# A list scheduler plans the first pass of layer one on every engine

## The chip, the cores and the metric

One core of a Trainium2 chip runs the kernel. The metric is the device time of one execution in microseconds (us), the median of several runs. Matrix products run on TensorE (PE; PEld is its weight load), reductions and elementwise work on VectorE (DVE), exponentials, tanh and copies on ScalarE (ACT). SyncE (SP) issues every DMA. Each engine works through its own queue in the order in which the program gives it.

## The reference, cut to what matters

```python
k_p = k.reshape(B, H, Sp, 8, D).mean(axis=3)          # B=8, H=8, D=64, 576 positions -> Sp=72
v_p = v.reshape(B, H, Sp, 8, D).mean(axis=3)
attn = softmax(q @ k_p.T / sqrt(D))                   # per batch and head
x = (attn @ v_p), heads side by side                  # 4608 tokens x 512
h = x @ w_in;  g = h / (1 + exp(-1.702 h));  y = g @ w_out     # layer one, d_ff 2048
out = ((y @ w_a) * (y @ w_b)) @ w_o2                  # layer two, d_ff 1536
```

The weights come in 64-bit floats and are converted on the chip into two 32-bit parts (hi, lo). Activations are split in the same way, and each product of layer one is three products, hi by hi, hi by lo and lo by hi.

## The kernel before

The 4608 tokens are 9 blocks of 512. A block has four units of 128 tokens, 36 units in all, and 4.5 units make a batch of the attention. Layer one runs in two passes over the blocks: the first takes `FIRST_FS` = 2, 3, 4, 5, 6, 6, ... chunks of 128 hidden columns of block 0, 1, 2, ..., 44 steps in all; the second pass takes the rest. A step is 12 products `h` (128x512), tanh on ACT, gate on DVE, hi on ACT, lo on DVE, and 12 products `acc` (the output y, four banks). Layer two follows. Attention for the units of a block runs in the first pass, between the steps of the block before it.

A unit's stages, with the lines of the profile: scores `sc` (PE, L286), maxima `mx` (DVE, L293), exponentials into `at` (ACT, L296), normalising (DVE, L308 to L310), transposes `pt` (PE, L318), their copies `aT` (ACT, L321), averages `px` (PE, L333), and x's hi part (ACT, L97) and lo part (DVE, L98), each in two halves of 256 columns. A batch needs the sums of k (`ks`, DVE L255, then `kbd` on ACT) and of v (`vs`, DVE L267), from loads `kraw`, `vraw` (`kvraw` for the first two batches), whose buffers are one and two. A weight chunk is loaded as `raw`, and converted on ACT and DVE (`tmp`, `w`, L120 to L139). A block's x is stored to memory (`xd`) for the second pass, in four transfers, and loaded there in four, `load_x` being issued five steps ahead.

What sets the order: the start is written out by hand (`in_order`, `keep_busy`), and from block 1's attention on, `spread` deals the attention's stages over the steps of the block before. `tc.issue_after` ties an operation to the newest DVE instruction; apart from that the framework orders an engine's instructions by its own estimate. `keep_busy(n)` issues n products of the identity with itself (`busy`, L170) so that TensorE does not stand idle:

```python
keep_busy(12)
in_order(*sk[0], b1(0)[0], b1(1)[0], b1(0)[1], b1(1)[1], *b1(2), sv[0][0])
keep_busy(8)
...
spread([o for t in ts for o in later[t]], place[0, j - 1, 0] - 1, place[0, j, 0] - 1)
```

A product of 32-bit operands (`busy`, `sc`, `px`) stands as two records in the trace; `pt` and the 128x512 products of layer one are one record each.

Of the kernel before, what the change touches and what calls it, by code (L numbers as in the profile page):

```python
# [20 lines left out]
LOW, HIGH = (struct.unpack("<f", struct.pack("<I", b))[0] for b in (0x38000000, 0x47EFFFFF))  # L21


@with_exitstack
def tile_kernel(ctx, tc, q, k, v, w_in, w_out, w_a, w_b, w_o2, out):
# [54 lines left out]
    newest = [None]  # L80

    def vec(made):
        newest[0] = made.ins
        return made

    def in_order(*ops):

        for o in ops:
            if newest[0] is None:
                o()  # L90
            else:
                with tc.issue_after(newest[0]):
                    o()

    def split(hi, lo, src):

        nc.scalar.copy(out=hi, in_=src)  # L97
        vec(nc.vector.tensor_tensor(out=lo, in0=src, in1=f32(hi), op=ALU.subtract))  # L98
# [15 lines left out]
    def convert(raw, t, hi, lo, part, first_on_act=False):  # L114
# [3 lines left out]
        if part == 0:  # L118
            if first_on_act:
                nc.scalar.activation(out=f32(t), in_=f32(high), func=AF.Abs)  # L120
            else:
                nc.vector.tensor_scalar(out=t, in0=high, scalar1=0x7FFFFFFF, scalar2=None, op0=ALU.bitwise_and)
# [5 lines left out]
            vec(nc.vector.scalar_tensor_tensor(  # L128
                out=t, in0=high, scalar=0xC0000000, in1=t, op0=ALU.bitwise_and, op1=ALU.bitwise_or
            ))  # L130
            nc.scalar.copy(out=hi, in_=f32(t))
            return
# [6 lines left out]
        vec(nc.vector.tensor_tensor(out=lo, in0=f32(t), in1=f32(low), op=ALU.add))  # L139

    def mm3(o, whi, wlo, xhi, xlo, first, last):
        nc.tensor.matmul(out=o, lhsT=whi, rhs=xhi, start=first, stop=False)  # L142
        nc.tensor.matmul(out=o, lhsT=whi, rhs=xlo, start=False, stop=False)  # L143
        nc.tensor.matmul(out=o, lhsT=wlo, rhs=xhi, start=False, stop=last)  # L144
# [74 lines left out]
    early = {}  # L219
    q_t, ks_t, vs_t, at_t, atT_t, kraw_t, vraw_t = {}, {}, {}, {}, {}, {}, {}  # L220
# [20 lines left out]


    scale = 1.0 / (POOL * D ** 0.5)

    def to_kbd(b, half, ks):


        cs = slice(2 * half, 2 * half + 2)
        nc.scalar.mul(out=kbd[b % 2][0:D, cs, 0:SP], in_=ks[0:D], mul=scale)
        nc.scalar.mul(out=kbd[b % 2][D:P, cs, SP:2 * SP], in_=ks[D:P], mul=scale)  # L250

    def sum_k(b, half):
        ks = ap_.tile([P, 2, SP], F32, tag="ks", name="ks", bufs=2)
        raw = kraw_t.pop((b, half)).rearrange("p c (s r) -> p c s r", r=POOL)
        vec(nc.vector.tensor_reduce(out=ks, in_=raw, op=ALU.add, axis=AX.X))  # L255
        to_kbd(b, half, ks)

    def load_v(b, h, n, raw=None):
        if raw is None:
            raw = ap_.tile([SP, n, D, POOL], F32, tag="vraw", name="vraw", bufs=2)  # L260
        nc.sync.dma_start(out=raw, in_=v[b, :, h:h + n])
        vraw_t[b, h] = raw

    def sum_v(b, h, n):
        if h == 0:
            vs_t[b] = ap_.tile([SP, H, D], F32, tag="vs", name="vs", bufs=2)
        vec(nc.vector.tensor_reduce(out=vs_t[b][:, h:h + n, :], in_=vraw_t.pop((b, h)), op=ALU.add, axis=AX.X))  # L267

    def stage_b1(u, half):
        qT = q_t[u]  # L270
        if half == 0:
            at_t[u] = (
                early["at"][:, u % 2] if UB > u >= UB // 2 else ap_.tile([P, H, SP], F32, tag="at", name="at", bufs=2),
# [3 lines left out]
        a, mx, sm = at_t[u]  # L277
        if (u, half) in ((2, 0), (2, 1), (3, 0)):
            sc = acc.tile([P, H // 2, SP], F32, tag="acc", name="sc")
        else:  # L280
            sc = ps.tile([P, H // 2, SP], F32, tag="ps", name="sc")
        pin = after_last if u < UB else lambda made: None
        for c in range(2):
            pair = 2 * half + c
            for o, n, b in pieces(u):
                pin(nc.tensor.matmul(  # L286
                    out=sc[o:o + n, 2 * c:2 * c + 2, :].rearrange("p h k -> p (h k)"),
                    lhsT=qT[:, pair, o:o + n],
                    rhs=kbd[b % 2][:, pair, :],
                    start=True, stop=True,  # L290
                ))
        hs = slice(half * (H // 2), (half + 1) * (H // 2))
        vec(nc.vector.tensor_reduce(out=mx[:, hs], in_=sc, op=ALU.max, axis=AX.X, negate=True))  # L293
        for c in range(H // 2):
            h = half * (H // 2) + c
            nc.scalar.activation(  # L296
                out=a[:, h, :], in_=sc[:, c, :], func=AF.Exp, bias=mx[:, h:h + 1],
                accum_out=sm[:, h:h + 1],
            )
        if half == 1:  # L300
            q_t.pop(u)
            if UB <= u + 2 < NU:
                load_q(u + 2)

    def stage_b2(u):
        a, _, sm = at_t[u]

        nc.vector.tensor_scalar(out=sm, in0=sm, scalar1=1e-9, scalar2=float(POOL), op0=ALU.add, op1=ALU.mult)  # L308
        nc.vector.reciprocal(out=sm, in_=sm)
        vec(nc.vector.tensor_tensor(out=a, in0=a, in1=sm.unsqueeze(2).to_broadcast([P, H, SP]), op=ALU.mult))  # L310

    def stage_c(u):
        a = at_t.pop(u)[0]
        aT = early["aT"][:, u // 2] if u in (1, 3) else ap_.tile([SP, H, P], F32, tag="aT", name="aT", bufs=1)
        for half in range(2):
            pt = ps.tile([SP, H // 2, P], F32, tag="ps", name="pt")
            for c in range(H // 2):
                made = nc.tensor.transpose(pt[:, c, :], a[:, half * (H // 2) + c, :], ident)  # L318
                if u < UB:
                    after_last(made)  # L320
            nc.scalar.copy(out=aT[:, half * (H // 2):(half + 1) * (H // 2), :], in_=pt)  # L321
        atT_t[u] = aT

    def stage_d(u):
        aT = atT_t.pop(u)
        j, c0 = u // UB, u % UB * P
        if (0, j) not in x_t:
            x_t[0, j] = x_tiles()
        px = ps.tile([P, NP, P], F32, tag="ps", name="px")
        for c in range(NP):  # L330
            for e in range(2):
                for o, w, b in pieces(u):
                    made = nc.tensor.matmul(  # L333
                        out=px[e * D:(e + 1) * D, c, o:o + w],
                        lhsT=vs_t[b][:, 2 * c + e, :],
                        rhs=aT[:, 2 * c + e, o:o + w],
                        start=True, stop=True,
                    )
                    if u < UB:
                        after_last(made)  # L340
        for h in range(2):
            hi, lo = x_t[0, j][0][h], x_t[0, j][1][h]
            split(hi[:, :, c0:c0 + P], lo[:, :, c0:c0 + P], px[:, 2 * h:2 * h + 2])
            if u % UB == UB - 1:
                nc.sync.dma_start(out=xd[j][:, 0, 2 * h:2 * h + 2], in_=f32(hi))
                nc.sync.dma_start(out=xd[j][:, 1, 2 * h:2 * h + 2], in_=f32(lo))
# [4 lines left out]


    def slot(t, lo, hi):

        todo = [
            (t, op(stage_b1, t, 0)), (t - 1, op(stage_b2, t - 1)), (t - 2, op(stage_d, t - 2)),
            (t, op(stage_b1, t, 1)), (t - 1, op(stage_c, t - 1)),
        ]
        return [o for u, o in todo if lo <= u < hi]

    slots = [slot(t, 0, UB) for t in range(UB + 2)]
    later = {t: slot(t, UB, NU) for t in range(UB, NU + 2)}
    V = 2
    for b in range(2, B):
        u0 = b * S // P
        for t, ops in (
            (u0 - 5, [op(load_k, b, 0)]), (u0 - 4, [op(sum_k, b, 0), op(load_k, b, 1), op(load_v, b, 0, V)]),
            (u0 - 3, [op(sum_k, b, 1), op(load_v, b, V, V)]),
            (u0 - 2, [op(sum_v, b, 0, V), op(load_v, b, 2 * V, V)]),
            (u0 - 1, [op(sum_v, b, V, V), op(load_v, b, 3 * V, V)]),  # L370
# [653 lines left out]
```

## Time and profile before

| | us |
|---|---|
| median of 3 runs | 1805.42 (1804.43 to 1808.48) |
| the profiled execution | 1805.87, its span 1804.1 |
| PE busy in the span | 1751.0 (97%) |
| DVE busy in the span | 1040.4 (58%) |
| ACT busy in the span | 607.1 (34%) |

The span is the stretch from the first to the last instruction that the profile holds; 1.8 us lie around it. Busy time of PE is modelled, so a busy PE is not PE at its best; the granted clock (PEclk) says whether it ran at its full 2.4 GHz (1.00) or at 1.2 GHz (0.50).

### The profile page before, as it was taken

What the parts mean: (1) busy time and instruction counts of PE and PEld (TensorE: products, weight loads), DVE (VectorE), ACT (ScalarE), POOL (GpSimd) and SP (SyncE); (2) the same over time, 40 slices, a digit from 0 to 9 for tenths busy, and PEclk for the clock granted to TensorE, in tenths of its full rate; (3) what the DMA queues carried; (4) which work ended last, traced back from release to release, by engine and by line L of the source; (5) the groups of instructions that cost most, each with busy time, mean ns of one, the idle gap of its engine ahead of it and who ended that gap; (6) DMA issues with size and microseconds to landing.
All of it is one profiled execution on the core that took longest, in us unless ns stands there. A gap on an engine that the chain in (4) does not pass through costs nothing.

```text
span 1804.1 us, 22540 instructions
## 1 busy us (share of the span) xinstructions
PE 1751.0 (97%) x8584; PEld 1443.2 (80%) x8584; DVE 1040.4 (58%) x1821; ACT 607.1 (34%) x1515; POOL 1.7 (0%) x8
## 2 busy tenths in 40 slices
PE   7779999999999999999999999999999999999998
PEld 6557788888888888888887788878788888788887
DVE  6877787667534768758755665733334443434343
ACT  5666665533222333323333232222221111221121
POOL 0000000000000000000000000000000000000000
PEclk8999999999999999999999999999999999999999
DMA  8475553353220644657587675768436659536612
GB/s 259 144 230 193 178 171 127 117 193 129 75 113 35 239 181 184 247 181 257 209 307 310 267 278 178 258 262 331 193 127 223 233 187 333 225 134 248 233 56 91
DMA packets 92171, 357.98 MB, mean 198 GB/s; under 512 B 10304, under 2 KB 10304, under 8 KB 71680
## 3 DMA queue, kind: packets, MB, share of 16 engines
q1 hardware_dynamic: 92064, 356.56, 54.8%
q8 instruction: 67, 1.10, 0.2%
q14 instruction: 40, 0.33, 0.1%
HBM read 238.55 MB, written 117.96 MB: 198 GB/s over the span
## 4 chain that ended last, share of the span: by engine, by line
PE 88%; DVE 5%; DMA 5%; ACT 1%; issue 0%; SPq 0%; ACTq 0%; DVEq 0%
PE X L516 16%; PE Y L516 8%; PE acc L143 7%; PE acc L144 7%; PE acc L142 7%; PE h L142 7%; PE h L144 7%; PE h L143 7%; PE acc L471 5%; PE acc L469 5%; PE acc L470 5%; PE Z L516 4%; DMA vraw<-in_v_dram 2%; PE px L333 1%; PE sc L286 1%; PE pt L318 1%
## 5 line engine op out<-in xcount | busy, mean ns | idle before, releaser
L516 PE MATMUL X<-xo,wc 128*128 128x512 f32 (+1 forms) x1440 | 330.3, 370 | 5.3 <-DVE s L534 4.5
L516 PEld LDWEIGHTS X<-xo,wc 128*128 128x128 f32 x1440 | 255.5, 189 | 58.7 <-DVE s L534 11.7
L143 PE MATMUL acc<-glo,w 128*128 128x512 f32 x576 | 227.4, 395 | 2.1 <-DVE glo L444 2.1
L142 PE MATMUL h<-x,w 128*128 128x512 f32 x576 | 225.7, 393 | 1.4 <-ACT aT L321 0.7
L144 PE MATMUL acc<-ghi,w 128*128 128x512 f32 x576 | 226.2, 394 | 0.0
L143 PE MATMUL h<-x,w 128*128 128x512 f32 x576 | 224.7, 390 | 0.0
L144 PE MATMUL h<-x,w 128*128 128x512 f32 x576 | 224.6, 390 | 0.0
L439 DVE SCALAR_TENSOR_TENSOR g<-g,h 128x512 f32<-128x512 f32 x144 | 98.5, 684 | 185.1 <-ACT g L436 185.0
L142 PE MATMUL acc<-ghi,w 128*128 128x512 f32 x576 | 176.1, 398 | 10.9 <-ACT ghi L440 7.1
L436 ACT ACTIVATE g<-h 128x512 f32<-128x512 f32 x144 | 86.2, 599 | 279.5 <-PE h L144 243.3
L516 PE MATMUL Y<-xo,wc 128*128 128x512 f32 (+1 forms) x720 | 167.4, 368 | 0.0
L501 ACT CAST ghi<-s 128x512 fp32r<-128x512 f32 (+1 forms) x60 | 34.7, 578 | 337.4 <-DVE s L535 337.4
L516 PEld LDWEIGHTS Y<-xo,wc 128*128 128x128 f32 x720 | 128.4, 189 | 23.7
L530 DVE TENSOR_TENSOR s<-s,Y 128x512 f32<-128x512 f32 (+1 forms) x60 | 38.0, 634 | 170.7 <-PE Y L516 170.3
L142 PEld LDWEIGHTS acc<-ghi,w 128*128 128x128 f32 x576 | 106.7, 189 | 33.9 <-ACT ghi L440 9.0
L143 PEld LDWEIGHTS acc<-glo,w 128*128 128x128 f32 x576 | 109.1, 189 | 25.8 <-DVE glo L444 3.0
L142 PEld LDWEIGHTS h<-x,w 128*128 128x128 f32 x576 | 108.3, 188 | 25.5 <-ACT aT L321 1.8
L144 PEld LDWEIGHTS acc<-ghi,w 128*128 128x128 f32 x576 | 109.3, 190 | 23.0 <-DVE w L139 0.6
L440 ACT CAST ghi<-g 128x512 fp32r<-128x512 f32 x144 | 89.7, 623 | 109.6 <-DVE g L439 76.9
L144 PEld LDWEIGHTS h<-x,w 128*128 128x128 f32 x576 | 108.2, 188 | 22.7 <-issue 0.2
L143 PEld LDWEIGHTS h<-x,w 128*128 128x128 f32 x576 | 108.3, 188 | 22.1 <-issue 0.2
L444 DVE TENSOR_TENSOR glo<-g,ghi 128x512 fp32r<-128x512 f32 x144 | 99.0, 687 | 36.8 <-ACT ghi L440 35.6
(90 smaller groups left out, 2521.4 us busy)
## 6 DMA issues: line engine op xcount, KB each, us to landing
xo<-yd SPq DMA_DIRECT2D x84, 1024.0 KB
yd<-st SPq DMA_DIRECT2D x28, 1024.0 KB
part<-part SPq DMA_DIRECT2D x108, 256.0 KB
xd<-x SPq DMA_DIRECT2D x36, 512.0 KB
part<-ys SPq DMA_DIRECT2D x72, 256.0 KB
x<-xd SPq DMA_DIRECT2D x36, 512.0 KB
raw<-in_moe_w_out_dram SPq DMA_DIRECT2D x28, 512.0 KB
wd<-ws SPq DMA_DIRECT2D x12, 1024.0 KB
```

Of the source, the lines that this page charges most:

```text
L142: nc.tensor.matmul(out=o, lhsT=whi, rhs=xhi, start=first, stop=False)
L143: nc.tensor.matmul(out=o, lhsT=whi, rhs=xlo, start=False, stop=False)
L144: nc.tensor.matmul(out=o, lhsT=wlo, rhs=xhi, start=False, stop=last)
L436: nc.scalar.activation(out=g, in_=hps, func=AF.Tanh, scale=0.5 * 1.702)
L439: made = vec(nc.vector.scalar_tensor_tensor(out=g, in0=g, scalar=1.0, in1=hps, op0=ALU.add, op1=ALU.mult))
L440: nc.scalar.copy(out=ghi, in_=g)
L444: return rest, lambda: vec(nc.vector.tensor_tensor(out=glo, in0=g, in1=f32(ghi), op=ALU.subtract))
L469: after_last(nc.tensor.matmul(out=oa, lhsT=chi[:, ts], rhs=whi, start=first, stop=False))
L470: after_last(nc.tensor.matmul(out=oa, lhsT=chi[:, ts], rhs=wlo, start=False, stop=False))
L471: after_last(nc.tensor.matmul(out=oa, lhsT=clo[:, ts], rhs=whi, start=False, stop=last))
L516: after_last(nc.tensor.matmul(out=banks[nm], lhsT=w[:, at_, we, ks], rhs=x[:, xe, kk, :], start=n in FIRST and kk == 0 and m == 0, stop=kk ...
L530: nc.vector.tensor_tensor(out=s[2], in0=s[2], in1=Y, op=ALU.add)
```

## The change

All work of the first pass (loads, attention, weight chunks 0 to 10, the 44 steps, their evictions and stores) becomes a table of tasks (`first_tasks`) with an engine, a cost, what it waits for, and the buffers that it takes and gives back. `first_plan` is a list scheduler in the source: it takes the task that can start earliest by its table, ties by the longest path to the end plus a bonus per kind (`LEAN`). The kernel emits the tasks in the order of the planned starts, and `pin` holds PE, ACT and DVE to that order. Up to the first y product, gaps that the plan leaves on PE are filled with `keep_busy`, six products for each us of gap (`FILL`). The copies `aT` become half buffers (three of them). x's hi and lo parts become whole tiles: one copy and one subtraction of 512 columns for each unit, a block's store and load two transfers of 1 MB in place of four. The first conversion step of chunks 6 to 10 moves from DVE to ACT, and the first three blocks' evictions are all ACT's (6 fewer on DVE in the pass).

```diff
+COST = dict(
+    k=1.51, q=.67, v=1.51, vq=.76, w=1.34, x=2.69, p=.67,
...
+DELAY = dict(PE=.30, ACT=.18, DVE=.18, SP=2.2)
+ROOM = dict(ps=4, acc=3, at=2, aT=3, tmp=2, g=1, gg=2, ks=2, kraw=1, vraw=2, q=2, xs=3, raw=2, yp=2, w=19)
...
+FILL = 6
+ACT_EVICTS = 3
...
+def first_tasks(counts, seq, chunks_made, per):
+
+    tasks = {}
+
+    def add(name, engine, kind, deps=(), takes=(), gives=()):
+        tasks[name] = (engine, kind, list(deps), list(takes), list(gives))
...
+            add(f"mx{u}.{e}", "DVE", "mx", [f"sc{u}.{e}"])
+            add(f"ex{u}.{e}", "ACT", "ex", [f"mx{u}.{e}"], (), [bank])
+        add(f"b2{u}", "DVE", "b2", [f"ex{u}.0", f"ex{u}.1"])
+        for e in range(2):
+            back = ([f"px{u - 1}.0"] if e else [f"px{u - 2}.1"]) if u >= per else [f"px{u - 2}.{e}"] if u >= 2 else []
+            add(
+                f"pt{u}.{e}", "PE", "pt", [f"b2{u}"] + back + ([f"pt{u}.0"] if e else []), [bank],
+                ([] if u == 2 else ["w"] if u == 3 else ["at"]) if e else [],
+            )
+            add(f"cp{u}.{e}", "ACT", "cp", [f"pt{u}.{e}"], ["aT"], [bank])
...
+def first_plan(tasks):
...
+        path[n] = COST[tasks[n][1]] + .2 + max([path[m] for m in after[n]], default=0.)
+    key = {n: -path[n] - LEAN.get(t[1], 0.) for n, t in tasks.items()}
+    room, ready, bank, start = dict(ROOM), {}, {}, {}
+    free = dict(PE=2.3, ACT=2.8, DVE=2.8, SP=.7)
...
+    while len(start) < len(tasks):
+        best = None
+        for e, names in queue.items():
+            for n in names:
+                s = max(free[e], ready[n], now)
+                if (best is None or (s, key[n], n) < best) and fits(tasks[n][3]):
+                    best = (s, key[n], n)
...
+        queue[engine].remove(n)
+        start[n] = s
+        free[engine] = s + COST[kind]
+        end = free[engine] + DELAY[engine]
+        for r in back:
+            heapq.heappush(gives, (end, bank[holder(n)] if r == "any" else r))
...
+    def pin(engine, made):
+
+        if engine in chain:
+            tc.add_manual_dep(
+                made.ins, chain[engine].name,
+                mybir.DependencyInfo(mybir.DependencyClass.NoSync, mybir.DependencyReason.DATA),
+                reason="order of the plan",
+            )
+        chain[engine] = made.ins
+        return made
...
     def load_x(i, j):
-        x_t[i, j] = x_tiles()
+        x_t[i, j], ts = x_tiles()
         for e in range(2):
-            for h in range(2):
-                nc.sync.dma_start(out=f32(x_t[i, j][e][h]), in_=xd[j][:, e, 2 * h:2 * h + 2])
+            nc.sync.dma_start(out=f32(ts[e]).rearrange("p h k n -> p (h k) n"), in_=xd[j][:, e])
 
...
+    def copy_aT(u, half):
+        aT_t[u, half] = ap_.tile([SP, H // 2, P], F32, tag="aT", name="aT", bufs=ROOM["aT"])
+        pin("ACT", nc.scalar.copy(out=aT_t[u, half], in_=pt_t.pop((u, half))))
...
+    def x_part(u, e):
+        j, c0 = u // UB, u % UB * P
+        if e == 0 and u % UB == 0:
+            x_t[0, j], x_full[j] = x_tiles()
+        hi, lo = (t.rearrange("p h k n -> p (h k) n")[:, :, c0:c0 + P] for t in x_full[j])
+        if e == 0:
+            pin("ACT", nc.scalar.copy(out=hi, in_=px_t[u]))
+        else:
+            pin("DVE", nc.vector.tensor_tensor(out=lo, in0=px_t.pop(u), in1=f32(hi), op=ALU.subtract))
+
+    def store_x(j, e):
+        nc.sync.dma_start(out=xd[j][:, e], in_=f32(x_full[j][e]).rearrange("p h k n -> p (h k) n"))
...
-                if c % 2 == 0:
-                    nc.scalar.mul(out=t, in_=sums[c], mul=0.5)
-                else:
-                    nc.vector.tensor_scalar_mul(t, sums[c], 0.5)
-                nc.sync.dma_start(out=part[1][j][:, c, :], in_=t)
...
-    keep_busy(12)
-    in_order(*sk[0], b1(0)[0], b1(1)[0], b1(0)[1], b1(1)[1], *b1(2), sv[0][0])
-    keep_busy(8)
-    in_order(b2(0))
-    c_(0)()
-    keep_busy(3)
-    in_order(sv[0][1], b2(1), *b1(3), b2(2), c0[0], d_(0))
...
+    n1 = place[1, 0, FIRST_FS[0]]
+    start, bank = first_plan(tasks := first_tasks(FIRST_FS, S, FA + HELD, UB))
...
+    names = sorted(does, key=len, reverse=True)
+    pe_free, filling = 2.3, True
+    for name in sorted(start, key=lambda n: (start[n], n)):
+        kind = next(k_ for k_ in names if name.startswith(k_))
+        if tasks[name][0] == "PE":
+            if kind == "y" and filling:
+                filling = False
+                busy.clear()
+            if filling:
+                keep_busy(int((start[name] - pe_free) * FILL))
+            pe_free = start[name] + COST[tasks[name][1]]
+        does[kind](*(int(n) for n in name[len(kind):].split(".")))
```

The order on PE at the start of the program. `busy` are the fill products, `qs` and `kbd` the queries and summed keys of the first units, `at` the exponentials. Before:

```order
L170 MATMUL busy<-ident 128x128 x12
L286 MATMUL sc<-kbd_135,qs 128x144 x12
L170 MATMUL busy<-ident 128x128 x8
L318 MATMUL pt<-ident,at 72x128 x8
L170 MATMUL busy<-ident 128x128 x3
L286 MATMUL sc<-kbd_135,qs 128x144 x4
L333 MATMUL px<-aT,vs 64x128 x8
```

And now:

```order
L338 MATMUL busy<-ident 128x128 x41
L466 MATMUL sc<-kbd_135,qs 128x144 x8
L338 MATMUL busy<-ident 128x128 x11
L466 MATMUL sc<-kbd_135,qs 128x144 x2
L338 MATMUL busy<-ident 128x128
L466 MATMUL sc<-kbd_135,qs 128x144 x2
L338 MATMUL busy<-ident 128x128 x12
L498 MATMUL pt<-ident,at 72x128 x4
```

The fill ahead of the first scores grows from 12 products to 41, and more stands between the first units. Ahead of the first h product the whole order holds 104 fill products where it held 32, and four more come after it; it also holds all scores of units 4 and 5 and the transposes of unit 4 there, which came after it before.

The order on DVE where the first sums of v from the small buffers `vraw` stand (batch 2). `ks` are sums of k, `mx` maxima, `sm` and `at` the normalising, `x` the lo parts. Before:

```order
L293 TENSOR_REDUCE mx<-sc 128x4
L255 TENSOR_REDUCE ks<-kraw 128x144
L293 TENSOR_REDUCE mx<-sc 128x4
L308 TENSOR_SCALAR sm<-sm 128x8
L309 RECIPROCAL sm<-sm 128x8
L310 TENSOR_TENSOR at<-at,sm 128x576
L98 TENSOR_TENSOR x<-px,x 128x2x128 x2
L293 TENSOR_REDUCE mx<-sc 128x4
L267 TENSOR_REDUCE vs<-vraw 72x128
```

And now, with `g` and `glo` of a step and `tmp` of a weight chunk among them:

```order
L528 TENSOR_TENSOR x<-px,x 128x4x128
L423 TENSOR_REDUCE ks<-kraw 128x144
L475 TENSOR_REDUCE mx<-sc 128x4
L1080 TENSOR_TENSOR glo<-g,ghi 128x512
L444 TENSOR_REDUCE vs<-vraw 72x128 x2
L1069 SCALAR_TENSOR_TENSOR g<-g,h 128x512
L475 TENSOR_REDUCE mx<-sc 128x4 x2
L584 TENSOR_SCALAR tmp<-tmp 128x512
```

The two sums now stand together between a step's lo part (`glo`) and the next step's gate (`g`), where each stood among a unit's normalising and maxima; the lo part of x is one instruction of 512 columns for a unit in place of two of 256.

The order of the loads on SP at the start. Before:

```order
L239 DMA kvraw<-in_k_dram 128x1152
L233 DMA qs<-in_q_dram 128x512
L239 DMA kvraw<-in_k_dram 128x1152
L233 DMA qs<-in_q_dram 128x512 x2
L261 DMA kvraw<-in_v_dram 72x2048 x2
L233 DMA qs<-in_q_dram 128x512
```

And now:

```order
L610 DMA raw<-in_moe_w_in_dram 128x1024
L417 DMA kvraw<-in_k_dram 128x1152 x2
L610 DMA raw<-in_moe_w_out_dram 128x1024
L409 DMA qs<-in_q_dram 128x512 x4
L409 DMA q<-in_q_dram 128x512 x2
L417 DMA kraw<-in_k_dram 128x1152
L437 DMA kvraw<-in_v_dram 72x2048
```

The first weight chunk goes ahead of k, and the first v comes behind the queries of six units.

## Rows read from the trace of the kernel before

**Rows 1.** Windows: length, busy time per engine (records), granted clock, DMA share, GB/s.

```profile
0.00:51.00 51.00, 37.81 (x235) 31.48 (x235) 34.86 (x59) 27.35 (x107) 1.73 (x8) 0.87 0.77 230
51.00:100.00 49.00, 36.23 (x260) 27.39 (x260) 38.13 (x69) 33.52 (x149) 0.00 (x0) 0.97 0.59 187
100.00:150.00 50.00, 41.65 (x296) 32.63 (x292) 40.48 (x75) 31.60 (x116) 0.00 (x0) 0.97 0.66 209
150.00:200.00 50.00, 45.84 (x267) 36.25 (x268) 38.40 (x77) 30.99 (x121) 0.00 (x0) 0.97 0.50 164
200.00:250.00 50.00, 49.04 (x313) 39.24 (x313) 36.05 (x72) 29.74 (x108) 0.00 (x0) 1.00 0.54 184
250.00:427.00 177.00, 177.00 (x1022) 145.06 (x1017) 117.84 (x237) 89.94 (x300) 0.00 (x0) 1.00 0.43 151
```

**Rows 2.** Timeline of PE, start: start, duration, records [idle before, releaser].

```profile
2.34 5.49 PE L170 MATMUL busy<-ident 128*128 128x128 f32 x24 [2.34 <-POOL ident masks.py:199]
7.62 1.06 PE L286 MATMUL sc<-kbd,qs 128*128 128x144 f32 x4
10.05 3.01 PE L286 MATMUL sc<-kbd,qs 128*128 128x144 f32 x20 [1.37 <-DMA qs<-in_q_dram]
12.90 1.95 PE L170 MATMUL busy<-ident 128*128 128x128 f32 x16
...
22.35 1.09 PE L333 MATMUL px<-aT,vs 72*64 72x128 f32 x16
23.37 1.07 PE L318 MATMUL pt<-ident,at 128*72 128x128 f32 x8
...
49.74 0.39 PE L142 MATMUL h<-x,w 128*128 128x512 f32 x1
49.97 0.40 PE L143 MATMUL h<-x,w 128*128 128x512 f32 x1
```

**Rows 3.** Waits of PE from 51 to 250: us in total, times, longest.

```profile
PE pt L318 <- DVE at L310: 11.3, 7, 3.9
PE acc L142 <- ACT ghi L440: 4.1, 3, 2.5
PE acc L142 <- ACT w L131: 3.6, 1, 3.6
```

**Rows 4.** Waits of DVE from 51 to 250.

```profile
DVE g L439 <- ACT g L436: 13.8, 7, 3.5
DVE vs L267 <- DMA vraw<-in_v_dram: 8.0, 8, 1.8
DVE ks L255 <- DMA kraw<-in_k_dram: 7.1, 3, 3.8
...
DVE ys L630 <- DMA part<-ys: 3.3, 1, 3.3
```

**Rows 5.** Chain that ended last, its DMAs from 88 to 126.

```profile
88.12 7.36 DMA vraw<-in_v_dram
96.75 9.02 DMA vraw<-in_v_dram
...
121.74 4.45 DMA kraw<-in_k_dram
```

**Rows 6.** Groups by line and shape: busy, mean ns of one | idle before.

```profile
L98 DVE TENSOR_TENSOR st<-part,st 128x512 fp32r<-128x512 f32 x63 | 41.8, 686 | 4.4 <-ACT st L97 4.2
...
L98 DVE TENSOR_TENSOR x<-px,x 128x256 fp32r<-128x256 f32 x72 | 30.0, 418 | 12.2 <-ACT x L97 11.8
...
L630 DVE TENSOR_SCALAR ys<-acc 128x512 f32<-128x512 f32 x18 | 12.4, 688 | 15.8 <-DMA part<-ys 15.5
...
L122 DVE TENSOR_SCALAR tmp<-raw 128x512 uint32<-128x512 uint32 x20 | 8.4, 421 | 0.0
L120 ACT ACTIVATE tmp<-raw 128x512 f32<-128x512 f32 x12 | 8.0, 671 | 12.1 <-DMA raw<-in_moe_w_in_dram 8.2 <-DMA raw<-in_moe_w_out_dram 2.6 <-DVE w L139 1.1
```

**Rows 7.** Windows at the start, the columns as in the first group.

```profile
0.00:10.00 10.00, 6.35 (x28) 6.10 (x28) 2.61 (x2) 2.13 (x4) 1.73 (x8) 1.00 0.80 247
10.00:20.00 10.00, 6.70 (x48) 6.27 (x49) 7.92 (x12) 8.11 (x51) 0.00 (x0) 0.93 1.02 281
```

More of the change, by code (lines that the diff above doesn't have):

```diff
@@ new lines, in holder, with fits @@
+def holder(name):
+    kind = name[:2]
+    if kind in ("sc", "ex"):
+        return "sc" + name[2:]
+    if kind in ("pt", "cp"):
+        return "pt" + name[2:]
+    return "px" + name[2:].split(".")[0]
+def first_plan(tasks):
+    after = {n: [] for n in tasks}
+    left = {n: len(t[2]) for n, t in tasks.items()}
+    for n, t in tasks.items():
+        for d in t[2]:
+            after[d].append(n)
+    todo, line = dict(left), [n for n in tasks if not left[n]]
+    for n in line:
+        for m in after[n]:
+            todo[m] -= 1
+            if not todo[m]:
+                line.append(m)
+    path = {}
+    for n in reversed(line):
+        path[n] = COST[tasks[n][1]] + .2 + max([path[m] for m in after[n]], default=0.)
+    key = {n: -path[n] - LEAN.get(t[1], 0.) for n, t in tasks.items()}
+    room, ready, bank, start = dict(ROOM), {}, {}, {}
+    free = dict(PE=2.3, ACT=2.8, DVE=2.8, SP=.7)
+    queue = {e: [] for e in free}
+    for n, t in tasks.items():
+        if not left[n]:
+            ready[n] = 0.
+            queue[t[0]].append(n)
+    now, gives = 0., []
+    def fits(takes):
+        return all(
+            room["ps"] > 0 or room["acc"] > 0 if r == "any" else room[r] >= takes.count(r) for r in takes
+        )
+    while len(start) < len(tasks):
[5 more added lines that the diff above has]
+                    best = (s, key[n], n)
+        if gives and (best is None or gives[0][0] <= best[0]):
+            now = max(now, gives[0][0])
+            while gives and gives[0][0] <= now:
+                room[heapq.heappop(gives)[1]] += 1
+            continue
+        s, _, n = best
+        engine, kind, _, takes, back = tasks[n]
+        now = max(now, s)
+        for r in takes:
+            if r == "any":
+                r = bank[holder(n)] = "acc" if room["acc"] > 0 else "ps"
+            room[r] -= 1
+        queue[engine].remove(n)
[4 more added lines that the diff above has]
+            heapq.heappush(gives, (end, bank[holder(n)] if r == "any" else r))
+        for m in after[n]:
+            left[m] -= 1
+            ready[m] = max(ready.get(m, 0.), end)
+            if not left[m]:
+                queue[tasks[m][0]].append(m)
+    return start, bank
@@ L258, in load_v @@
[L258 to L265, printed above, removed]
[L266 to L270 removed]
+        pin("DVE", nc.vector.tensor_reduce(out=ks, in_=raw, op=ALU.add, axis=AX.X))
@@ L312, in stage_c @@
[L312 to L330, printed above, removed]
+            ))
+    def normalise(u):
+        a, _, sm = at_t[u]
+        pin("DVE", nc.vector.tensor_scalar(out=sm, in0=sm, scalar1=1e-9, scalar2=float(POOL), op0=ALU.add, op1=ALU.mult))
+        pin("DVE", nc.vector.reciprocal(out=sm, in_=sm))
+        pin("DVE", nc.vector.tensor_tensor(out=a, in0=a, in1=sm.unsqueeze(2).to_broadcast([P, H, SP]), op=ALU.mult))
@@ L337, in stage_d @@
                         start=True, stop=True,
[L338 to L346, printed above, removed]
+                    ))
@@ L728, in tile_kernel @@
     J9 = NB - 1
-    spread_late(ahead(late[:HELD]), place[0, 4, 1], place[0, J9, 1])
     spread_late(ahead(late[HELD:]), place[0, J9, 2], place[1, 0, FA + HELD])
-    for f in range(2, FA):
-        j = f - 1
-        todo[place[0, j, 0] - 1].append(op(load_w, (1, f)))
     w2_t, raws, vs2 = {}, {}, {}
@@ new lines, in g_lo, with y_product @@
+    def g_lo(j, f):
+        ghi, glo = g_t[0, j, f]
+        pin("DVE", nc.vector.tensor_tensor(out=glo, in0=h_t.pop((j, f, "g")), in1=f32(ghi), op=ALU.subtract))
+    def y_product(j, f, c):
+        s, fs = (0, j, f), chunks(0, j)
+        if c == 0:
+            if place[s] + 1 == n1:
+                first(steps[n1])
+            begin(s)
+        ghi, glo = g_t[s]
+        w, cs = w_t[1, f], slice(c * P, (c + 1) * P)
+        mm3(sums[0, j][c], w[:, 1, cs], w[:, 3, cs], ghi, glo, f == fs[0], f == fs[-1])
+        if c == 3:
+            g_t.pop(s)
+            for o in todo[place[s]]:
+                o()
+            if f == fs[-1]:
+                x_t.pop((0, j))
@@ L953, in tile_kernel @@
+    early.clear()
+    planned[0] = False
     p2x = ExitStack()
```

404 lines of the change are left out of this document (237 added, 167 removed).

## The prediction

> **What bounds the kernel now.** I read the windows first, since the change touches only the first pass of layer one. They show where that pass loses time: from 250 us on PE is busy for all of 177 us at full clock, and DVE is at 67% [rows 1]. There a shift of work to or from the other engines is worth nothing; the end is PE's own work. Before 250 us PE is not full. From 51 to 250 us its busy time adds up to 172.8 of 199 us, so 26.2 us are idle, and the granted clock of 0.97 over 149 us, a mean of its two levels 1.2 and 2.4 GHz, costs about 4.5 us more [rows 1]. That is 30.7 us lost, and 168.3 us of full-speed work. Up to 51 us the start is latency: loads, sums, scores, exponentials, transposes, averages, then the first h.
>
> The waits of PE say who keeps it in the middle stretch: the normalised exponentials (`at`, 11.3 us) and the hi part of g (4.1), both products of DVE's and ACT's queues, and one conversion of a weight chunk (3.6) [rows 3]. DVE in turn is busy for 153.1 of these 199 us [rows 1] and waits for tanh (13.8) and for DMAs: v 8.0, k 7.1, the stores of y 3.3 [rows 4]. So neither engine is full there; they wait for each other in the order in which their queues stand, and for loads. The chain that ended last runs through the same loads, with 7.36 and 9.02 us of v and 4.45 us of k [rows 5].
>
> **The change part by part.**
>
> The start. What counts is how much useful PE work is done when. Before, at 51 us, units 0 to 3 are through attention, h and y of step 0 are done, the second step's first two products are issued [rows 2], and a few scores of unit 4. At the durations of the rows this is 32 score records of 0.15 us, 32 transposes of 0.134, 64 records of averages of 0.068 [rows 2], 26 products at 0.227 (49.97 less 49.74, [rows 2]) and some 1.7 us of scores: 21 us. After the change the order has ahead of the end of the first h: 56 score records (8.4 us), 40 transposes (5.4), 64 records of averages (4.4) and 12 products (2.7), also 21 us. But it also has 104 fill products in place of 32. A fill product is two records. At the clock of the second group of fills it takes 1.95/8 = 0.244 us; in the first group, 5.49/12 = 0.458 us [rows 2]. So 104 cost 25.4 us at full clock. PE had been busy with them since 2.34 us; its scores at 7.62 still take 0.265 us a record and those from 10.05 on 0.15 [rows 2], so the first 7.7 us go at the lower level, which costs another 17 x 0.214 = 3.6 us. With the start at 2.34 us the first h ends at 2.3 + 20.9 + 25.4 + 3.6 = 52.2 us, if PE never waits. The fill is six products, 1.46 us, for each us that the plan sees idle, so it overruns the gaps that it fills, and there is little left to wait for: the first eight loads are 3.3 MB, the first v comes after 5.0 MB, and at the 247 and 281 GB/s of the start [rows 7] these are there at about 13 and 19 us, while the fill ahead of the first scores alone takes until 15.7 us (17 x 0.458 and 24 x 0.244 from 2.34). Result: after has done at 52.2 us what before has done at 51. The start costs 1.2 us. The four fills behind the first h cost 1.0 us.
>
> The middle. From there to the point that before reaches at 250 us the useful work is the same 168.3 us. If the planned order kept PE full, 30.7 us would go; if it only traded waits for others, nothing. What a new order can't take away by itself are waits for transfers, since `kraw` and `vraw` keep one and two buffers, and the plan reckons a load of k at 1.5 and of a part of v at 0.76 us plus 2.2, where the chain shows 4.45 and up to 9.02 [rows 5]. Those waits at DVE were 8.0 + 7.1 + 3.3 = 18.4 us [rows 4]. DVE idled 45.9 us for PE's 26.2, so 0.57 us of a DVE wait reaches PE; 18.4 x 0.57 = 10.5 us. I take this as what stays, between nothing and all of 30.7.
>
> DVE's work. A whole lo part has no row from this source; the nearest of 512 columns are the lo part of a stored operand at 686 ns, and below it one half's 418 [rows 6]. I take 0.69: 36 x 0.69 = 24.8 in place of 30.0 us, 5.2 saved (15 at the lower end). Ten first conversion steps go to ACT: 10 x 0.421 = 4.2 us off DVE, 10 x 0.671 onto ACT [rows 6]. Six evictions go: 6 x 0.688 = 4.1 us. These 13.5 us I cost at nothing in the end time, because DVE needs at most its 153 us in a stretch that would now last some 180, 85% of it; they are room. If DVE became the bound they would be worth up to their share of that stretch, about 6 us. ACT is at 126 of 199 us [rows 1], and takes about 6.7 + 3.6 us more over the whole pass, for which it has the room. The half copies `aT` are as many as before; their third buffer and the split averages only ease a wait.
>
> x's parts whole: of 9 x 8 transfers 36 fall away on SP, whose issue nobody on PE waits for [rows 3]: nothing. The load for the second pass is issued five steps ahead, 5 x 24 x 0.227 = 27 us, and a first product that must now see all of a part waits for 0.5 MB more, 2 us at 247 GB/s [rows 7]: hidden, for the 18 parts 36 us if that cover were gone. The Trainium skill ("Perfetto Trace Analysis", section DMA Optimizations) speaks against this part: split transfers may let some work start sooner when the DMA engines are mostly idle. By that rule the sum would lose up to those 36 us; by the rows of waits, where no PE wait is on x, it loses none.
>
> The sum: 30.7 - 10.5 - 1.2 - 1.0 = 18.0 us gained. The profiled execution took 1805.9 us, 0.4 above the median, so 1788 us. From 250 us of before on, the same work follows at a full PE, so nothing is given back there.
>
> **The rivals.**
>
> All waits go: 30.7 - 2.2 = 28.5 us, 1777. For it speaks that DVE's 153 us fit into 168 at 91%, and that 13.5 us leave it; against it the loads. Were the fill never at the lower clock, 3.6 us more: 1774.
>
> No change: the waits only move. PE's and DVE's queues are now both fixed by costs and by a plan in which the first h comes earlier than the fill lets it, so each late task holds what stands behind it. The same comes out if TensorE stays at the lower level through all fills: 104 x 0.458 = 47.6 in place of 29.0 us, and the other 21 us at half rate, which takes the whole 30. Against the latter: the second group of fills is at 0.122 a record [rows 2]. Time 1802 to 1809.
>
> Slower: a late load stops DVE for everything. The stretch has 24 sums of v and 12 of k in the small buffers over the pass, which now stand ahead of a step's gate on DVE. At a mean wait of 1.0 us each (8.0/8 in the rows, up to 3.8 for k [rows 4]), all reaching PE since nothing else is left to do, 36 us replace the 30.7: 1805.9 + 36 + 2.2 - 30.7 = 1813. It decides from a mean of 0.8 us on. Against it: the small buffers' loads now have other DVE work of several us between two sums that share a buffer. The Trainium skill ("TensorE: Matmul & The Clock Gate", section on the array's architectural detail) calls the queues of ScalarE and VectorE strictly first in, first out; by that rule this rival would hold whenever a load is late, and the trace agrees in so far as 8 of DVE's waits for v stand in it [rows 4].
>
> **How the numbers follow.** The forecast, 1777 to 1802 with 1788 as its likeliest, gets 0.66; all waits gone, under 1777, 0.08; no change 0.12; slower 0.14. About 0.2% (3.6 us) is what a measurement of this kernel can tell from no change. Faster is 0.66 + 0.08 = 0.74; of the no-change case a little lies above that bound, so same 0.11 and slower 0.15. The range goes from 1775, just under the case without waits, to 1810, into the slower one; about 0.06 lie below and 0.12 above.
>
> **What would show it.** Right: the first h ends at 50 to 54 us; over a hundred fill products ahead of it, most at 0.122 us a record; PE's idle time from there on near 10 us, most of it behind DVE sums that wait for loads; gap-free PE from about 230 us on. Wrong: idle PE of 25 us or more after the first h (the slower or the equal rival), a granted clock of 0.50 between 15 and 50 us, or waits of PE for `x` in the second pass. A first h well before 50 us would show the price of the fill wrong.

## The result and the profile after

| | before | after |
|---|---|---|
| median, us | 1804.93 (1802.7 to 1808.48, 4 runs) | 1779.62 (1779.54 to 1781.9, 4 runs) |
| the profiled execution, us | 1805.87, span 1804.1 | 1781.9, span 1780.1 |
| PE busy, rest of the span, us | 1751.0, 53.1 | 1759.9, 20.2 |

The ratio is 0.9861 with a 95% interval of 0.9843 to 0.9879: faster by 25.3 us, where the forecast was 18. In the profiled executions the span is shorter by 24.0 us: 32.9 us of PE's idle time are gone, and PE is busy for 8.9 us more. 76 more fill products, some 17 us at 0.224 us each, are among its work, and less of the other work runs at the lower clock: the granted clock stood at 0.50 in six stretches of the pass before, in which PE was busy for 21.9 us, and stands there in one of 3.4 us now (69.9 to 73.3 us).

The page of the changed kernel, its part on busy time:

```profile
PE 1759.9 (99%) x8736; PEld 1450.6 (81%) x8736; DVE 1036.3 (58%) x1769; ACT 613.6 (34%) x1495; POOL 1.7 (0%) x8
```

Its windows (the columns as in [rows 1]), cut at 51 us as before and at the end of its first h product:

```profile
51.00:250.00 199.00, 194.64 (x1215) 153.26 (x1216) 176.26 (x310) 140.92 (x504) 0.00 (x0) 0.99 0.65 216
```

```profile
47.20:100.00 52.80, 51.01 (x372) 39.98 (x371) 47.95 (x88) 41.18 (x150) 0.00 (x0) 0.97 0.68 226
47.20:250.00 202.80, 198.44 (x1272) 156.48 (x1271) 179.64 (x317) 144.28 (x515) 0.00 (x0) 0.99 0.64 215
```

From 51 to 250 us PE is idle for 4.4 us, where it was idle for 26.2 [rows 1]. DVE does more in the same stretch (176.3 us, where it was 153.1), because the pass comes forward: all engines work more tightly. Nearly all of the gain is made in the first pass, 22.4 of the 24.0 us: that is how much sooner the `glo` of its last step starts. Before, then after:

```profile
421.56 0.69 DVE L444 TENSOR_TENSOR glo<-g,ghi 128x512 fp32r<-128x512 f32 x1
```

```profile
399.18 0.69 DVE L1080 TENSOR_TENSOR glo<-g,ghi 128x512 fp32r<-128x512 f32 x1
```

PE's timeline at the start, as in [rows 2]:

```profile
2.35 12.33 PE L338 MATMUL busy<-ident 128*128 128x128 f32 x82 [2.35 <-POOL ident masks.py:199]
14.51 2.13 PE L466 MATMUL sc<-kbd,qs 128*128 128x144 f32 x16
16.47 2.62 PE L338 MATMUL busy<-ident 128*128 128x128 f32 x22
18.93 0.66 PE L466 MATMUL sc<-kbd,qs 128*128 128x144 f32 x4
...
22.81 0.60 PE L498 MATMUL pt<-ident,at 128*72 128x128 f32 x4
23.25 0.39 PE L338 MATMUL busy<-ident 128*128 128x128 f32 x2
...
44.20 0.47 PE L302 MATMUL h<-x,w 128*128 128x512 f32 x1
...
46.82 0.40 PE L304 MATMUL h<-x,w 128*128 128x512 f32 x1
47.06 0.66 PE L466 MATMUL sc<-kbd,q 128*128 128x144 f32 x4
```

No row of this view up to 47 us, shown or not, has a wait behind it but the first: the fill closes every gap, and the first h ends at 47.1 us, 5.1 us sooner than forecast.

The waits of PE from 0 to 420 us, and those of DVE from 51 to 250 (as [rows 3] and [rows 4]):

```profile
PE sc L466 <- DVE g L1069: 2.6, 1, 2.6
PE busy L338 <- POOL ident masks.py:199: 2.3, 1, 2.3
PE sc L466 <- ACT at L482: 1.6, 1, 1.6
```

```profile
DVE g L1069 <- ACT g L1065: 9.0, 7, 4.1
DVE ys L1104 <- DMA part<-ys: 3.4, 1, 3.4
DVE x L528 <- ACT x L526: 2.3, 5, 0.9
```

The 11.3 us behind `at`, PE's greatest wait, are gone, and so is every wait of DVE for k and v (15.1 us in [rows 4]). ACT's waits for weight chunks (`raw`) in that stretch are gone too, 8.5 us before; its waits for the stores of y grew from 1.5 to 4.0 us. The view of the tile `vraw` from 51 to 250 us lists the idle time ahead of its instructions and finds none:

```profile
L444 DVE TENSOR_REDUCE vs<-vraw x20: 1204/1205/1210, 71.1 to 242.4; 72x128 f32<-72x1024 f32 x20
L437 SPq DMA_DIRECT2D vraw<-in_v_dram x20: 321/326/1984, 75.2 to 243.7; - x20
its engine sat idle before it (us, times) until:
who waited for it (us, times):
```

Why is seen on SP and DVE around one pair of v's sums. The timelines of SP and of DVE:

```profile
75.23 0.35 SPq L437 DMA_DIRECT2D vraw<-in_v_dram  x1
...
76.69 0.39 SPq L437 DMA_DIRECT2D vraw<-in_v_dram  x1
```

```profile
71.11 2.33 DVE L444 TENSOR_REDUCE vs<-vraw 72x128 f32<-72x1024 f32 x2
...
85.91 2.33 DVE L444 TENSOR_REDUCE vs<-vraw 72x128 f32<-72x1024 f32 x2
```

The loads are issued 1.8 and 3.2 us after the pair of sums before has freed the two buffers, and the next pair begins on DVE 10.7 and 9.2 us behind their issue, with other work between. The transfers of before that held the chain took up to 9.02 us [rows 5]. This pair is a roomy one: the closest sum of the stretch stands 5.6 us behind the issue of its load (173.9 and 179.5 us), and it doesn't wait either.

The longest wait of PE that is left in the pass hangs on a store. The chain that ended last, around 140 us:

```profile
139.74 7.99 DMA part<-ys
147.88 0.45 issue
148.33 0.60 ACT g L1065
148.95 0.70 DVE g L1069
149.69 0.76 PE sc L466 x4
```

An eviction on ACT waits for the store of an earlier y to free its buffer, ACT's tanh stands behind the eviction, DVE's gate behind tanh, and PE's scores behind the gate.

### The profile page after: what moved, and what is told of

Its sections match the earlier page's. It is cut to its first block, busy times and chain, and to the rows that moved or that the text cites. A ratio compares the mean times of both kernels' runs of the same rounds, so it can differ in the third digit from the quotient of the medians.

```text
span 1780.1 us, 22762 instructions
## 1 busy us (share of the span) xinstructions
PE 1759.9 (99%) x8736; PEld 1450.6 (81%) x8736; DVE 1036.3 (58%) x1769; ACT 613.6 (34%) x1495; POOL 1.7 (0%) x8
## 4 chain that ended last, share of the span: by engine, by line
PE 94%; DVE 2%; DMA 2%; ACT 1%; issue 0%; POOL 0%; POOLq 0%; ACTq 0%; DVEq 0%; SPq 0%
PE X L707 16%; PE Y L707 8%; PE acc L302 8%; PE h L302 7%; PE acc L303 7%; PE acc L304 7%; PE h L303 7%; PE h L304 7%; PE acc L662 5%; PE acc L660 5%; PE acc L661 5%; PE Z L707 4%; PE px L513 2%; PE sc L466 2%; DMA part<-ys 2%; PE pt L498 2%
## 5 line engine op out<-in xcount | busy, mean ns | idle before, releaser
L304 PE MATMUL acc<-ghi,w 128*128 128x512 f32 x576 | 224.7, 390 | 0.0
L302 PE MATMUL acc<-ghi,w 128*128 128x512 f32 x576 | 198.1, 410 | 0.0
L630 DVE SCALAR_TENSOR_TENSOR g<-g,h 128x512 f32<-128x512 f32 x100 | 68.5, 685 | 151.0 <-ACT g L627 151.0
L627 ACT ACTIVATE g<-h 128x512 f32<-128x512 f32 x100 | 59.8, 598 | 228.9 <-PE h L304 190.7
L302 PEld LDWEIGHTS acc<-ghi,w 128*128 128x128 f32 x576 | 108.2, 188 | 26.2 <-issue 7.9
L482 ACT ACTIVATE at<-sc,mx 128x72 f32<-128x72 f32 x288 | 88.2, 333 | 21.3 <-DVE mx L475 21.2
L768 DVE TENSOR_TENSOR part<-acc,part 128x512 f32<-128x512 f32 x72 | 49.7, 692 | 78.8 <-PE acc L662 64.2
```

Of the source, the lines that this page charges most:

```text
L482: pin("ACT", nc.scalar.activation(out=a[:, h, :], in_=sc[:, c, :], func=AF.Exp, bias=mx[:, h:h + 1], accum_out=sm[:, h:h + 1],))
L627: nc.scalar.activation(out=g, in_=hps, func=AF.Tanh, scale=0.5 * 1.702)
L630: made = (nc.vector.scalar_tensor_tensor(out=g, in0=g, scalar=1.0, in1=hps, op0=ALU.add, op1=ALU.mult))
L768: nc.vector.tensor_tensor(out=t, in0=a, in1=t, op=ALU.add)
```

## The experiments

The theory after the result (A): the planned order of DVE and ACT, with a delay reckoned behind each load, took away the waits; the fill, the whole parts of x and the tuned bonuses are small. The rivals (B or C in the texts): the fill and TensorE's clock; the order on PE; x's parts.

**The fill, none.** Edit: `-FILL = 6`, `+FILL = 0`.

> The planned order without any fill product (the six per us become none). Theory A, the order on all engines makes the gain and the fill only stands in time that PE would idle: 1775 to 1785 us; the first h comes within 4 us of the 44.2 us of the change, since without fill the first scores can start near 10 instead of 14.5 us, but the granted clock falls to 0.50 between the bursts. Theory B, the fill makes the gain by keeping the clock up: at least half of the 25 us is lost, 1792 us or more.

1781.01 us (1776.64 to 1783.8), ratio 0.9861 (0.984 to 0.9881). Windows, and waits of PE from 0 to 51:

```profile
0.00:51.00 51.00, 26.30 (x175) 22.08 (x176) 34.25 (x55) 29.72 (x126) 1.73 (x8) 0.83 0.77 238
51.00:250.00 199.00, 195.80 (x1261) 154.06 (x1260) 178.70 (x316) 143.36 (x515) 0.00 (x0) 1.00 0.64 218
```

```profile
PE pt L498 <- DVE at L492: 12.6, 2, 8.4
PE sc L466 <- DMA qs<-in_q_dram: 10.2, 1, 10.2
```

Without fill PE idles for 24.7 us up to 51 at a granted clock of 0.83, and the time is the same. The first h starts at 47.21 us, 3.0 later than with the fill. PE waits for the queries and for the normalising where it had fill to do.

**The fill, four products for each us.** Edit: `-FILL = 6`, `+FILL = 4`.

> The planned order with four fill products for each us of planned gap in place of six, which at 0.244 us each is one us for each us. Theory A with a fill that overruns its gaps: the first scores come about 3 us sooner, the first h up to 5 us sooner, and the time is 1774 to 1779 us. If the overrun costs nothing, because the engines behind it have other work to do in the meantime, 1779 to 1781. Theory B (fill makes the gain): 1782 us or more.

1780.53 us (1777.17 to 1787.69), ratio 0.9868 (0.9845 to 0.989). The first h starts at 42.86 us, 1.3 us sooner, and that is lost in the noise. That six products overrun their gaps costs nothing that can be measured.

**The fill in the kernel before.** Edit: `keep_busy(12)` becomes `keep_busy(41)`, `keep_busy(8)` becomes `keep_busy(24)`.

> The kernel before, with 41 fill products in place of 12 ahead of the first scores and 24 in place of 8 behind the scores of units 0 to 2; everything else as before. Theory A (the order on DVE and ACT and the reckoning of loads carry the gain, the fill does nothing for it): no faster than before, 1803 to 1815, the first h later by up to 10 us than before's. Rival B (what the longer fill does to TensorE's granted clock carries part of the gain): the clock of 0 to 51 us rises from 0.87 to near 1.00 and the time falls to 1790 to 1800.

1814.86 us (1813.25 to 1817.2), ratio 1.0048 (1.003 to 1.0067): slower by some 9 us. The granted clock up to 51 us rises from 0.87 to only 0.90, and the first h moves from 36.67 to 45.86 us. Behind that the clock falls, from 0.97 to 0.92:

```profile
0.00:51.00 51.00, 40.19 (x296) 36.60 (x296) 25.86 (x46) 22.95 (x92) 1.73 (x8) 0.90 0.75 223
51.00:250.00 199.00, 172.39 (x1093) 135.09 (x1094) 151.81 (x284) 124.32 (x488) 0.00 (x0) 0.92 0.55 180
```

More fill in a start that isn't planned around it brings nothing, and it delays what stands behind it; how much of the 9 us is the delay and how much the lower clock later, the run doesn't part. Since it did not bring the clock near 1.00, rival B falls by the run without fill and not by this one.

**Only PE held to the plan.** DVE and ACT are ordered by the framework.

```diff
-        if engine in chain:
+        if engine == "PE" and engine in chain:
```

> The plan's order is held on PE alone; on ACT and DVE the framework orders the same tasks by its own estimate. Theory A: the waits of PE for DVE and ACT come back, at least 8 us of them, 1788 to 1800 us. Rival C, the gain is less work and larger pieces and not the order on DVE and ACT: 1779 to 1783 us.

1817.76 us (1815.99 to 1819.93), ratio 1.0072 (1.0048 to 1.0096): slower than before, and further than either theory went. Waits from 51 to 250 us of PE, then of DVE:

```profile
PE pt L498 <- DVE at L492: 11.6, 4, 5.3
PE pt L498 <- DVE sm L490: 3.2, 1, 3.2
```

```profile
DVE mx L475 <- PE sc L466: 13.3, 10, 5.1
DVE sm L490 <- ACT at L482: 6.8, 7, 2.8
```

PE waits for the normalising as it did before [rows 3], and DVE for PE's scores: two queues in different orders wait for each other. Loads are little of it (`vraw` 3.4 us, `kraw` 1.6). But more than half of the loss is made earlier. PE's timeline at the start:

```profile
30.87 1.04 PE L498 MATMUL pt<-ident,at 128*72 128x128 f32 x4 [8.37 <-DVE sm L491]
...
62.68 0.47 PE L302 MATMUL h<-x,w 128*128 128x512 f32 x1
```

PE stands for 8.37 us ahead of the first transposes, again for the normalising, and the first h starts 18.5 us later than in the changed kernel, of the 34.1 us between the two profiled executions.

**PE and DVE held to it, ACT not.**

```diff
-        if engine in chain:
+        if engine != "ACT" and engine in chain:
```

> The planned kernel, with TensorE and DVE held to the plan and ACT ordered by the framework. With TensorE alone held to it the kernel took 1817.8, against 1779.6 with all three. Theory A (DVE's place of the sums and of the normalising among the gates is what counts): 1780 to 1790, most of the 38 us come back. Rival B (ACT's order counts as much, since DVE waits for ACT's copies and exponentials): 1795 to 1812.

1785.17 us (1781.78 to 1789.28), ratio 0.9886 (0.9862 to 0.991). Of the 38 us that the run before lost, DVE's order brings back 33. ACT's order, with the other two held, is worth at most some 5, and the intervals overlap. What ACT's order would bring without DVE's was not tried.

**Loads reckoned as almost immediate.** Edit: in `DELAY`, `SP=2.2` becomes `SP=0.2`. The plan, and so the order on all engines, is made again.

> The plan reckons 0.2 us of delay behind each transfer in place of 2.2, so sums of k and v may stand right behind their loads. If the plan's reckoning removed DVE's waits for loads (18.4 us before, none for k and v after), they come back here, 8 us or more at DVE, and the time is 1784 to 1795 us. If the loads are early anyway, since their buffers come free long before: fewer than 3 us of such waits and 1778 to 1783 us.

1800.12 us (1795.86 to 1802.79, 10 runs), ratio 0.9972 (0.9959 to 0.9986): 20.5 us of the 25.3 are lost, beyond both ranges expected. Waits of DVE from 51 to 250 us, its timeline at one of them, and PE's timeline at the start:

```profile
DVE vs L444 <- DMA vraw<-in_v_dram: 11.3, 3, 4.7
```

```profile
181.53 2.33 DVE L444 TENSOR_REDUCE vs<-vraw 72x128 f32<-72x1024 f32 x2
187.85 2.34 DVE L444 TENSOR_REDUCE vs<-vraw 72x128 f32<-72x1024 f32 x2 [3.21 <-DMA vraw<-in_v_dram]
```

```profile
2.34 10.05 PE L338 MATMUL busy<-ident 128*128 128x128 f32 x74 [2.34 <-POOL ident masks.py:199]
...
16.45 2.26 PE L466 MATMUL sc<-kbd,qs 128*128 128x144 f32 x8 [4.06 <-ACT tmp L582]
```

Two pairs of v's sums stand 6.3 us apart, and the second waits for its load, and all of DVE's queue behind it. Without that wait they would stand some 3.1 us apart. The same two pairs stand 8.0 us apart in the changed kernel (170.0 and 178.0 us), and neither waits. At the start ACT waits for a weight chunk that was planned too early (the view of its waits has 8.4 us for `raw`), with the scaling of k behind it, and PE stands for 4.06 us. The first h comes at 51.10 us, 6.9 later than in the changed kernel; from there to 400 us PE idles for 11.4 us, where it idled for 5.0. These are 13.3 of the 19.2 us between the profiled executions; so the idle time behind the first h, where DVE's waits for v lie, is one part of the loss, the late start is another of its size, and some 6 us are not placed.

**Loads reckoned as slower.** Edit: `SP=2.2` becomes `SP=5.0`.

> The plan reckons 5.0 us of delay behind each transfer in place of 2.2. If the plan's reckoning of the loads decides how well they are hidden, this is the more careful plan: no wait of DVE for a load, 1777 to 1782 us. If the order as tuned is what counts, 1782 to 1790 us.

1782.68 us (1780.42 to 1784.5), ratio 0.9879 (0.9861 to 0.9897), with no wait of DVE for k or v. This is the control for the run above: a plan made again, with bonuses that were not tuned for it, costs about 3 us, with overlapping intervals; 0.2 costs 20. Too late a reckoning is nearly free, too early a one is not.

**No bonuses.** Edit: `- LEAN.get(t[1], 0.)` becomes `- 0.`.

> The plan without its table of bonuses per kind: ties go by the longest path alone. Theory A, any list order by ready times on all engines removes most of the waits: 1780 to 1790 us. Rival D, the gain sits in the tuned table: 1795 us or more.

1783.41 us (1782.36 to 1789.5), ratio 0.9891 (0.987 to 0.9911). The tuned table is worth 4 to 5 us at most: the intervals overlap.

**x's copy and subtraction in halves, in the changed kernel.** Two of 256 columns each, in the planned places; the transfers stay whole.

```diff
+        for h in range(2):
+            cs, src = slice(2 * h, 2 * h + 2), px_t[u][:, 2 * h:2 * h + 2]
...
-            pin("DVE", nc.vector.tensor_tensor(out=lo, in0=px_t.pop(u), in1=f32(hi), op=ALU.subtract))
+                pin("DVE", nc.vector.tensor_tensor(out=lo[:, cs], in0=src, in1=f32(hi[:, cs]), op=ALU.subtract))
```

> The planned order with x's parts made in two halves of 256 columns again, 36 more instructions each on ACT and DVE (about 6 us on each), stores and loads still whole. Theory A: hidden, 1779 to 1783 us. Rival C, less DVE work makes a good part of the gain: 1785 us or more.

1782.79 us (1781.47 to 1785.67), ratio 0.9877 (0.9858 to 0.9896). With 72 subtractions of 415 ns in place of 36 of 685 on DVE, 29.9 us in place of 24.7, the time rises by 3.2, with overlapping intervals: 0 to 3 us.

**x's parts whole, in the kernel before.** One copy, one subtraction and whole stores and loads, as in the change, and nothing else of it.

```diff
-        for h in range(2):
-            hi, lo = x_t[0, j][0][h], x_t[0, j][1][h]
-            split(hi[:, :, c0:c0 + P], lo[:, :, c0:c0 + P], px[:, 2 * h:2 * h + 2])
...
+        split(hi[:, :, c0:c0 + P], lo[:, :, c0:c0 + P], px)
```

> The kernel before with x's parts whole (one copy and one subtraction of 512 columns for a unit, stores and loads of 1 MB), nothing planned. Theory A: 1801 to 1806 us, since DVE and ACT wait for each other there and not for work. Rival C, whole parts bring a good part of the gain: 1798 us or less.

1795.97 us (1790.71 to 1798.76), ratio 0.995 (0.9932 to 0.9968): against theory A, 9 us faster than before.

**The same, with four transfers of 512 KB for each store and load.**

```diff
-            nc.sync.dma_start(out=f32(ts[e]).rearrange("p h k n -> p (h k) n"), in_=xd[j][:, e])
+            for h in range(2):
+                nc.sync.dma_start(out=f32(x_t[i, j][e][h]), in_=xd[j][:, e, 2 * h:2 * h + 2])
```

> The kernel before with x's parts whole in the instructions (one copy and one subtraction of 512 columns for each unit) but with the four transfers of 512 KB for each store and load. It tells where the 9 us come from that whole parts brought by themselves in the kernel before. Theory A (36 instructions fewer on each of ACT and DVE, 5 us of DVE's time, and the order that the framework then gives): 1793 to 1799, as with whole transfers. Rival B (the transfers, fewer issues and fewer landings to wait for): back to 1803 to 1808.

1795.04 us (1793.4 to 1800.07), ratio 0.9943 (0.9925 to 0.9962). So some 9 us come with the instructions, not with the transfers. DVE and ACT each have 36 instructions fewer, the first h starts at 31.90 us with whole transfers and 33.29 with four, where it was 36.67, PE idles for 15.0 and 16.4 us from 51 to 250 us, where it was 26.2, and the framework also orders PE's queue otherwise. Which of the two, the shorter work or the order that came with it, brings the 9 us stays open.

**Stores reckoned as slower.** The plan counts 4 us more until a store of y frees its buffer.

```diff
-        end = free[engine] + DELAY[engine]
+        end = free[engine] + DELAY[engine] + (4. if kind == "p" else 0.)
```

> The planned kernel, with the plan reckoning 4 us more until a store of y gives its buffer back (ROOM yp). In the planned kernel's trace the longest idle time of TensorE behind the first h, 2.6 us near 148 us, hangs on an eviction of y that waits for such a store, and DVE waits 3.4 us for one. Theory A (the plan's reckoning of a transfer removes a wait for it): these waits go, 1775 to 1779. Rival B (the evictions then stand later and the accumulators come free later): 1780 to 1786.

1781.8 us (1780.72 to 1783.3), ratio 0.9865 (0.9847 to 0.9883): the same. From 51 to 250 us DVE no longer waits for a store (3.4 us in the changed kernel) and ACT for 2.9 us (4.0), but DVE waits 2.6 us for `vraw`. PE is idle for 4.5 us of that stretch, as in the changed kernel. Fewer waits for stores bought PE nothing. No run beats the changed kernel.

## Why the prediction came out as it did

**The stretch and the mechanism: right.** "That is 30.7 us lost" named the stretch, and the gain came from there: PE's idle time from 51 to 250 us fell from 26.2 to 4.4 us. Both rivals on the other side of the gain fell. No late load stops DVE, and the waits did not just move. But the slower rival's mechanism is real, as the run with loads reckoned at 0.2 us shows: the strict queue that it rested on makes 11.3 us out of three late loads of v. The plan's reckoning decides whether it occurs.

**What failed is "18.4 x 0.57 = 10.5 us. I take this as what stays".** I put v, k and y's stores there, because the buffers stayed as few and the plan's 2.2 us lay under the 4.45 to 9.02 of the chain. Measured: k and v 0, a store 3.4 us at DVE, where it was 3.3, and at ACT 4.0 us for stores, which I had not counted. Few buffers fix the earliest time of a load, not that of the sum. The plan puts each sum behind its load. It asks only for 0.76 + 2.2 us between them; at the pair in the rows above the other tasks make it 10.7, and at the closest 5.6. So the middle of the forecast lay too far towards the waits that stay: the rival "all waits go" with 1777 lies 2.6 us from the result, the forecast's middle 8.4.

**The start: mis-sized by 5 us.** "52.2 us, if PE never waits": PE never waited, and it was 47.1. I took durations of groups, in which the end of one overlaps the start of the next. From start to start, 22 fill records take 18.93 - 16.47 = 2.46 us, 0.224 us a product and not 0.244; 16 score records 1.96 us, 0.1225 each and not 0.15; 4 transposes 0.44, 0.11 each and not 0.134. For 63 fills, 56 scores and 40 transposes that is 1.3 + 1.5 + 1.0 = 3.8 us; the first 41 fills took 12.16 us (14.51 - 2.35) where I had 13.6, another 1.4. Together 5.2. The same overlap lies in my price of before's work at 51 us, so that before stood some 0.7 us ahead at that point and not level (18.7 us of useful work to 18.0, with 0.062 a record for averages).

**The sum made again** for the profiled executions. Up to the first h: 5.1 less 0.7, 4.4 better than forecast. The middle, from 47.2 to 250 us: idle 202.8 - 198.4 = 4.4, the clock of 0.97 over 52.8 us about 1.6, four fills 0.9, together 6.9 where I had 10.5 + 1.0; 4.6 better. 18.0 + 4.4 + 4.6 = 27.0, and 24.0 were measured. About 3 us don't close. The clock's share is not the cause: before's three stretches at 0.50 between 51 and 250 us, with PE busy for 9.0 us of them, cost 4.5 us, as I had. Counted over the whole pass it closes better: PE idles for 7.3 us up to 402 where it idled for 39.4 up to 427, 32.1 less; at half speed 21.9 and 3.4 us of busy time cost 9.3 us less; 76 more fills cost 17.0. That makes 24.4, and 0.8 us less idle time behind the pass makes 25.2 for the 24.0 measured. So I look for the open part in the split at the first h; no view settles it.

**DVE's saved work at nothing: right within what was tried.** The 5.2 us of x's lo parts are worth 0 to 3 us in the changed kernel. The conversion steps, the evictions and the half copies `aT` were not tried alone. **x's whole transfers at nothing: right.** PE has no wait for `x` in the second pass, and four transfers or two make no difference in the kernel before (1795.04 and 1795.97). The Trainium skill ("Perfetto Trace Analysis", section DMA Optimizations) says that splitting may help where the DMA engines are mostly idle; here they are busy for 0.54 to 0.76 of each window up to 250 us, and no run shows a gain from splitting. What I did not see is that the whole instructions alone are worth 9 us in the unplanned kernel. Costs and gains here don't add: what the plan gains includes what this edit gains without it.

**"What would show it"**: over a hundred fill products ahead of the first h, right, at 0.112 a record and not 0.122; PE without gaps from 150 us on, but for 0.6 us, and not from 230; its idle time behind the first h 5.0 us and not near 10, and none of it behind DVE sums that wait for loads; the first h well before 50 us, which the text had named as the sign of a wrong price for the fill, and was.

## What to carry to other kernels

An order that is held on one engine must be held on the engine that it trades work with: holding PE alone to the plan was worse than no plan, and DVE's order gave 33 of the 38 us back, while ACT left to the framework cost at most 5. In a planner, reckon a load late rather than early: 5.0 us cost 3 at most, 0.2 us cost 20. Price PE's work by the distance of starts, not by durations, and don't take the waits of one order for a floor of the next: few buffers fix when a load can start, not when its reader has to stand in the queue.

## What was not expected of the hardware

The windows give a granted clock of 1.00 at the start, and the records of the products say otherwise. The changed kernel's fill, PE busy since 2.35 us, in windows of 2 us, and its first two windows of 10 us:

```profile
4.00:6.00 2.00, 2.00 (x11) 2.00 (x11) 1.16 (x3) 0.66 (x1) 0.00 (x0) 1.00 1.01 403
6.00:8.00 2.00, 2.00 (x11) 2.00 (x11) 2.00 (x3) 0.94 (x2) 0.00 (x0) 1.00 1.00 404
8.00:10.00 2.00, 2.00 (x18) 2.00 (x17) 1.97 (x4) 1.54 (x5) 0.00 (x0) 1.00 1.05 404
10.00:12.00 2.00, 2.00 (x20) 2.00 (x20) 1.27 (x2) 0.00 (x0) 0.00 (x0) 1.00 1.07 400
```

```profile
0.00:10.00 10.00, 7.65 (x42) 7.66 (x43) 5.12 (x8) 4.62 (x9) 1.74 (x8) 1.00 0.83 318
10.00:20.00 10.00, 10.00 (x89) 10.00 (x89) 5.47 (x9) 4.30 (x29) 0.00 (x0) 1.00 1.05 321
```

Eleven records in 2 us become twenty (one at the edge of a window counts on both sides). From start to start the first 24 fill records of the kernel before take 7.62 - 2.34 = 5.28 us [rows 2], 0.22 each, and the later ones of the changed kernel 0.112: half the rate at first. The 1.00 of the first windows is no reading. In both traces the record of the clock begins only at 8.5 us, and a window without a record shows 1.00. So near the start the rate of the products is the better witness; half the rate fits 1.2 GHz, which no record there shows.

The loads move 318 and 321 GB/s in the first two windows of 10 us, where before's start moved 247 and 281 [rows 7]; which part of the new order of loads does that was not tried.
